# A Fourier mixing layer and a low-rank mixer in one kernel: weights and the second batch's rows asked for in another order

## The chip, the cores and the metric

The kernel runs on one core of one Trainium2 chip. The metric is the time of one launch in device microseconds (us). Three runs of the kernel before gave 485.04, 485.25 and 488.07 us; their median is 485.25 us. One further execution was taken with the hardware profiler: it took 485.87 us, of which 484.1 us lie between its first and its last instruction (the span). All times in this document that are given as a point ("at 49.10") count from the start of that span.

## The reference

For each of 8 batches, x is 3136 rows by 256 columns of float32.

```python
X = np.fft.fft(x, axis=1); X = np.fft.fft(X, axis=2)
x = X.real                                   # 8 x 3136 x 256
xt = x.transpose(0, 2, 1)
h = xt @ U @ V                               # U: 3136 x 32, V: 32 x 3136
u = x + h.transpose(0, 2, 1)
ch = np.maximum(u @ w_ch1, 0.0) @ w_ch2      # 256 -> 1024 -> 256
out = u + ch
```

## The kernel before, in words

The transforms are matrix products with tables of sines and cosines, which the kernel makes itself. The work has three stages.

**Setup.** VectorE (DVE) works out phases (helper `phase`, L184 to 188), ScalarE (ACT) takes sines of them (L190 to 200) and mirrors parts of the tables, GpSimd (POOL) mirrors others (L284). `fold_u` (L214, matmuls of L223) and `transform_u` (L239, matmuls of L249 and L262) put the columns of U into the tables.

**Folding and transforming one batch.** The rows of a batch lie in SBUF twice, in order (`xf`) and from the end (`xr`), each in two halves a = 0 and 1 of 98 partitions by 8 rows; one more partition (number 98) holds the single row of each half that has no partner. `fold` (L335) makes sums and differences: `along_d` (DVE, L319 and L321) folds the columns, `alone` (POOL, L325) copies the two columns without a partner, `mirror` (DVE, L328) joins `xf` and `xr`, `half` (DVE, L332) joins the two halves into the operand `G`. `seq` (L349, matmuls of L368) transforms along the rows, `chan` (L477, matmuls of L482 and L484) along the columns, `lowrank` and `last_row` (L489, L503) make the small operands `TA` and `VA` of the low-rank product.

**Chunks.** The 25088 rows of all batches are cut in 49 chunks of 512. `front(c)` (L521) adds the low-rank part (matmuls of L527) to the transform on DVE (L535), which gives `u`, and has `u` turned by a DMA transpose (`ut`, L538). `first_product(c, j)` (L541) multiplies by a block of `W1` (L547) and ACT applies the maximum (L549), `second_product(c, t)` (L551) multiplies by `W2` (L563), and DVE adds `ut` (L569, L571, L572) before the result is stored.

The order is written out by hand up to the loop's second chunk: everything in the setup, batch 0 and the first chunk stands in program order on each engine. The main loop (L731) issues products chunk by chunk; the steps that fold and transform batch 1 and later are spread over it by due slots (`spread`, L714): the fold of batch 1 over slots 4 to 22, its transform from slot 23 on, eight slots to a chunk. Each engine executes its own list strictly in order, so a DVE instruction that waits for a load holds back every DVE instruction behind it.

**The loads that matter here.** A DMA issued from POOL goes to one software queue, from SP to a hardware queue. Before the change POOL issues, in this order: `W1`'s first half with a cast to bfloat16 (L653), its second half as a gather in float32 to `w1t` (L55, cast later by POOL at L684), `V` (L658), `W2` with a cast (L659; the DRAM side is read in runs of 256 elements), then batch 1: `xr` half 0 (L73), `xf` half 0 (L55, a gather), `xr` half 1, `xf` half 1, and at the end the single rows of both halves of `xf` in one DMA (L77) and of `xr` in one DMA (L83). Early in the setup POOL also zeroes and fills `alt`, `TA[0]`, `TA[1]` and `VA[0]` (L172 to L182).

Of the kernel before, what the change touches and what calls it, by code (L numbers as in the profile page):

```python
# [11 lines left out]
FP32 = mybir.dt.float32  # L12
I32 = mybir.dt.int32
# [3 lines left out]
P = 128  # L17
PQ = 98
KP = PQ + 1
NI = 8  # L20
# [7 lines left out]
def kernel(  # L28
# [9 lines left out]
    nc = tc.nc  # L38
    B, S, D = x.shape
    R = moe_U.shape[1]  # L40
    H = moe_w_ch1.shape[1]
    JT = H // P
    HALF = S // 2
# [6 lines left out]
    gen = setup.enter_context(tc.tile_pool(name="gen", bufs=2))  # L50
    psum = ctx.enter_context(tc.tile_pool(name="psum", bufs=1, space=bass.MemoryType.PSUM))

    def gather(out_, t, rows, idx, w, off):

        nc.gpsimd.indirect_dma_start(  # L55
            out_, None, bass.AP(t.tensor, t.offset, [[w, rows], [1, w]]),
            bass.IndirectOffsetOnAxis(idx, 0), element_offset=off)

    def rev(t, b, a, w):

        return bass.AP(t.tensor, t.offset + (b * S + S - 784 - a * HALF) * w,
                       [[8 * w, PQ], [1, 8 * w]])

    xf = cpool.tile([KP, 2, NI, D], FP32, name="xf")
    xr = cpool.tile([KP, 2, NI, D], FP32, name="xr")

    def load_f(b, a):
        gather(xf[:PQ, a].rearrange("p i d -> p (i d)"), x, B * S // 8 - 1,
               xidx[:PQ, b, a:a + 1], 8 * D, D)

    def load_r(b, a):
        q = nc.sync if b == 0 else nc.gpsimd
        q.dma_start(out=xr[:PQ, a].rearrange("p i d -> p (i d)"), in_=rev(x, b, a, D))  # L73

    def load_0f(t, dst_f, b, w, q):
        lo = t.offset + b * S * w
        q.dma_start(out=dst_f[PQ:KP],  # L77
                    in_=bass.AP(t.tensor, lo + (NI - 1) * w,
                                [[w, 1], [HALF * w, 2], [-w, NI], [1, w]]))

    def load_0r(t, dst_r, b, w, q):
        lo = t.offset + b * S * w
        q.dma_start(out=dst_r[PQ:KP].rearrange("p a i d -> p a (i d)"),  # L83
                    in_=bass.AP(t.tensor, lo, [[w, 1], [HALF * w, 2], [1, NI * w]]))

    def load_half(b, a):
        load_f(b, a)
        load_r(b, a)
        if a == 1:
            load_0f(x, xf, b, D, nc.gpsimd)  # L90
            load_0r(x, xr, b, D, nc.gpsimd)
# [19 lines left out]
    pcol = gen.tile([P, 1], FP32, tag="pcol", name="pcol", bufs=1)  # L111
    load_0f(moe_U, UF, 0, R, nc.scalar)
    load_0r(x, xr, 0, D, nc.scalar)
    for t, n0, step in ((UF, 1, HALF), (UR, S - 784, -HALF)):
        nc.sync.dma_start(out=t[:PQ].rearrange("p a i d -> p a (i d)"),
                          in_=bass.AP(moe_U.tensor, moe_U.offset + n0 * R,
                                      [[8 * R, PQ], [step * R, 2], [1, 8 * R]]))
    load_0r(moe_U, UR, 0, R, nc.sync)
    load_r(0, 0)
    load_0f(x, xf, 0, D, nc.sync)  # L120
# [16 lines left out]
    EOF_ = cpool.tile([KP, 2, NI, 258], BF16, name="eof")  # L137
    EOR_ = cpool.tile([KP, 2, NI, 258], BF16, name="eor")
# [20 lines left out]
    W1 = cpool.tile([P, 2, H], BF16, name="w1")  # L159
    W2 = cpool.tile([P, JT, D], BF16, name="w2")  # L160
    VA = [cpool.tile([P, S], BF16, name=f"va{s}", tag=f"va{s}") for s in range(2)]
    TA = [cpool.tile([P, 256], BF16, name=f"ta{s}", tag=f"ta{s}") for s in range(2)]
    pint = cpool.tile([P, 1], I32, name="pint")
    alt = cpool.tile([P, 256], BF16, name="alt")
# [4 lines left out]
    def signs_along(t):  # L169

        v = t.rearrange("p (l two) -> p l two", two=2)
        nc.gpsimd.memset(v[:, :, 0:1], 1.0)  # L172
        nc.gpsimd.memset(v[:, :, 1:2], -1.0)

    signs_along(alt)
    for s in range(2):
        nc.gpsimd.memset(TA[s][:].bitcast(I32), 0)
        signs_along(TA[s][R:R + 2])
        nc.gpsimd.memset(TA[s][R:R + 1, :], 0.0)
        nc.gpsimd.memset(TA[s][R:R + 1, 0:1], 1.0)  # L180
        nc.gpsimd.memset(TA[s][R:R + 1, P:P + 1], -1.0)
    nc.gpsimd.memset(VA[0][:].bitcast(I32), 0)  # L182

    def phase(y, a_ap, col_ap, bits):  # L184

# [10 lines left out]
    def cosine(out_, y, bits):  # L196
        pp = y.shape[0]
        ab = gen.tile(list(y.shape), FP32, tag="ab", name="ab")
        nc.scalar.activation(ab[:], y, AF.Abs, bias=c_half[bits][:pp])
        nc.scalar.activation(out_, ab[:], AF.Sin, scale=TWO_PI / 2 ** bits, bias=c_nhp[:pp])  # L200
# [110 lines left out]
    def pin(ins):  # L311

        if PIN:
            tc.keep_in_program_order(ins)

    def along_d(a, src, dst, part):
        lo, hi = src[:, a, :, 1:128], src[:, a, :, 255:128:-1]
        if part == 0:
            pin(nc.vector.tensor_tensor(dst[:, a, :, 1:128], lo, hi, op=AL.subtract))  # L319
        else:  # L320
            pin(nc.vector.tensor_tensor(dst[:, a, :, 129:256], lo, hi, op=AL.add))  # L321

    def alone(a, src, dst):

        pin(nc.gpsimd.tensor_copy(dst[:, a, :, 128:257:128], src[:, a, :, 0:129:128]))  # L325

    def mirror(a, cols, op):
        pin(nc.vector.tensor_tensor(EOS[:, a, :, cols], EOF_[:, a, :, cols],  # L328
                                    EOR_[:, a, ::-1][:, :, cols], op=op))

    def half(b, par, cols):
        pin(nc.vector.tensor_tensor(G[b % 2][par][:, :, cols], EOS[:, 0, :, cols],  # L332
                                    EOS[:, 1, :, cols], op=AL.add if par == 0 else AL.subtract))

    def fold(b):  # L335

        for a in range(2):
            for src, dst in ((xf, EOF_), (xr, EOR_)):
                yield lambda a=a, src=src, dst=dst: (alone(a, src, dst),
                                                     along_d(a, src, dst, 0))  # L340
                yield lambda a=a, src=src, dst=dst: along_d(a, src, dst, 1)
            if b + 1 < B:
                yield lambda a=a: load_half(b + 1, a)
            yield lambda a=a: mirror(a, slice(0, 128), AL.subtract)
            yield lambda a=a: mirror(a, slice(128, 258), AL.add)
        for par in range(2):
            yield lambda par=par: half(b, par, slice(0, 258))
# [51 lines left out]
    def column_zeros():  # L399
        nc.gpsimd.memset(cf[:], 0.0)  # L400
        nc.gpsimd.memset(cr[:], 0.0)
# [87 lines left out]
    def lowrank(b):  # L489
# [3 lines left out]
        for typ in range(2):  # L493
            for par in range(2):
                nc.tensor.matmul(pt[:], d["tab"][:, typ, par, :], MDT[typ][:],  # L495
                                 start=(n == 0), stop=(n == 3 and b < B0))
# [152 lines left out]
    alone(0, xf, EOF_)  # L649
    nc.gpsimd.iota(pint[:], pattern=[[0, 1]], base=D, channel_multiplier=-1)  # L650
    nc.gpsimd.memset(pint[0:1], P)
    alone(1, xr, EOR_)
    nc.gpsimd.dma_start(out=W1[:, 0, :], in_=moe_w_ch1[0:P, :])  # L653
    w1t = gen.tile([P, H], FP32, name="w1t", tag="w1t", bufs=1)
    gather(w1t[:], moe_w_ch1, D, pint[:], H, 0)
    alone(1, xf, EOF_)
    signs_along(MSN[0:1])
    nc.gpsimd.dma_start(out=VA[0][:R, :], in_=moe_V)  # L658
    nc.gpsimd.dma_start(out=W2[:], in_=moe_w_ch2.rearrange("(j p) d -> p j d", p=P))  # L659

    for part in range(2):
        along_d(0, xr, EOR_, part)
# [6 lines left out]
        step()  # L669
    cosine(MC[:], pd[:], 17)  # L670
    MDT = [MSN, MC]
    along_d(1, xr, EOR_, 0)
    along_d(1, xf, EOF_, 0)
    mirror(1, slice(0, 128), AL.subtract)
# [2 lines left out]
    mirror(1, slice(256, 258), AL.add)  # L677
    for par in range(2):
        half(0, par, slice(256, 258))
    load_r(1, 0)  # L680
    load_f(1, 0)
    along_d(1, xr, EOR_, 1)
    load_r(1, 1)
    nc.gpsimd.tensor_copy(W1[:, 1, :], w1t[:])  # L684
    along_d(1, xf, EOF_, 1)
    mirror(1, slice(128, 256), AL.add)
    for par in range(2):
        half(0, par, slice(128, 256))
    load_f(1, 1)
    load_0f(x, xf, 1, D, nc.gpsimd)  # L690
    load_0r(x, xr, 1, D, nc.gpsimd)
    column_zeros()
    for par in range(2):
        nc.gpsimd.memset(G[1][par][:, :, 258:GW].bitcast(I32), 0)
# [24 lines left out]
    for b in range(1, B):  # L719
        hi = 8 * (b * S // CH - 1) + 2  # L720
        if b == 1:
            spread(list(fold(b)), 4, 23)
            spread(list(transform(b)), 23, hi)
        else:
            spread(list(fold(b)), hi - 66, hi - 35)
            spread(list(transform(b)), hi - 33, hi)
        if b == B0:
            spread(list(column_steps()), hi - 34, hi - 22)
# [46 lines left out]
```

## Time and profile before

| what | value |
|---|---|
| median of three runs | 485.25 us |
| the profiled execution, launch to end | 485.87 us |
| its span | 484.1 us |
| TensorE (PE) busy | 461.5 us, 95% of the span |
| DVE busy | 318.4 us, 66% |
| ACT busy | 282.6 us, 58% |
| POOL busy | 69.2 us, 14% |
| mean granted TensorE clock | 0.989 |
| DMA | 67.24 MB, mean 139 GB/s |

How to read it: a row of the timeline gives start, duration, engine, line of the kernel, operation, the output and the inputs with their shapes, and in square brackets how long the engine had been idle before and what ended that. "PEld" is TensorE's loading of weights. "SPq" or "POOLq" is an engine's queue of issued work. A row of the stage table gives for each engine the busy time and the number of instructions, then the granted TensorE clock, the mean busy share of the 16 DMA engines, and the traffic. A row of the list of DMA issues ends with the median time from issue to landing.

### The profile page before, as it was taken

Reading aid. Unit: us, or ns where it says so; the run is one execution under the profiler, and the core shown is the slowest. Engines: PE = TensorE matmul, PEld = TensorE weight load, DVE = VectorE, ACT = ScalarE, POOL = GpSimd, SP = SyncE. Lnnn points to the kernel's source line nnn. Section 1 sums busy time; section 2 is a strip of 40 time slices with the busy share of each in tenths; the row PEclk is TensorE's granted clock in tenths of the full one; section 3 lists DMA queues with packets and bytes.
Section 4 is the critical chain, followed back from the end, with each engine's and each line's share of the span. In section 5 each row is a group of like instructions: output and inputs, shape, how many; then the busy total and the mean of one; then the engine's idle time right before and its main releaser. Section 6 shows DMA issues by size and latency. Waiting matters only on the chain.

```text
span 484.1 us, 7947 instructions
## 1 busy us (share of the span) xinstructions
PE 461.5 (95%) x2979; PEld 294.9 (61%) x3033; DVE 318.4 (66%) x713; ACT 282.6 (58%) x532; POOL 69.2 (14%) x122
## 2 busy tenths in 40 slices
PE   3799799999999999999999999999999999999997
PEld 2444466665566666666666666666666666666665
DVE  8996979684668657775568657684678543434333
ACT  6826344765666556655566556655566556656562
POOL 8780421110022000130022001120000000000000
PEclk9979899999999999999999999999999999999999
DMA  7599999895266834784376725775324233343433
GB/s 209 126 207 181 160 211 172 160 184 108 66 187 182 208 66 116 182 190 130 89 196 176 182 66 144 186 205 106 88 65 118 81 85 90 86 107 96 126 89 129
DMA packets 103606, 67.24 MB, mean 139 GB/s; under 512 B 73546, under 2 KB 100068, under 8 KB 100416
## 3 DMA queue, kind: packets, MB, share of 16 engines
q1 hardware_dynamic: 97722, 40.69, 38.5%
q0 software_dynamic: 5824, 26.03, 19.9%
q8 instruction: 23, 0.38, 0.3%
q14 instruction: 15, 0.12, 0.1%
q10 hardware_dynamic: 22, 0.02, 0.0%
HBM read 29.33 MB, written 25.69 MB: 114 GB/s over the span
## 4 chain that ended last, share of the span: by engine, by line
PE 87%; DVE 7%; DMA 4%; issue 2%; POOL 0%; DVEq 0%; POOLq 0%
PE p L563 36%; PE p L547 32%; PE pt L368 9%; PE ph L527 4%; DMA xf<-in_x_dram 4%; PE pst L482 2%; PE pst L484 2%; PE ptt L495 1%; DVE eor L319 1%; PE ptc L453 1%; DVE eos L328 1%; DVE phe L188 1%; DVE pho L188 1%; DVE eof L321 0%; DVE eor L321 0%
## 5 line engine op out<-in xcount | busy, mean ns | idle before, releaser
L549 ACT ACTIVATE h<-p 128x512 bf16<-128x512 f32 x392 | 224.9, 599 | 158.3 <-PE p L547 148.8
L547 PE MATMUL p<-u,w 128*128 128x512 bf16 x732 | 209.4, 380 | 4.0 <-DVE u L535 3.1
L563 PE MATMUL p<-w,h 128*128 128x256 bf16 x1568 | 203.9, 273 | 1.5
L563 PEld LDWEIGHTS <-h 128*128 128x128 bf16 x1568 | 153.5, 98 | 60.1 <-issue 0.7
L547 PEld LDWEIGHTS <-w 128*128 128x128 bf16 x784 | 75.7, 98 | 56.8 <-DVE u L535 3.2
L569 DVE TENSOR_TENSOR o<-p,ut 128x4 f32<-128x4 f32 (+1 forms) x100 | 16.4, 164 | 92.7 <-PE p L563 87.3
L368 PEld LDWEIGHTS <-g 98*128 98x128 bf16 (+1 forms) x288 | 28.5, 99 | 28.1 <-issue 2.0
L375 DVE TENSOR_TENSOR tab<-pt,ev 128x32 bf16<-128x32 f32 x32 | 6.1, 192 | 57.5 <-PE pt L368 55.1
L55 POOL DMA_INDIRECT xf<-in_x_dram,xidx x16 | 17.9, 1120 | 167.2 <-DVE eof L321 160.8
L572 DVE TENSOR_TENSOR o<-p,ut 128x254 f32<-128x254 f32 (+1 forms) x100 | 40.8, 408 | 0.0
L571 DVE TENSOR_TENSOR o<-p,ut 128x254 f32<-128x254 f32 (+1 forms) x100 | 40.8, 408 | 0.0
L368 PE MATMUL pt<-tabc,g 98*128 98x425 bf16 (+1 forms) x160 | 35.5, 349 | 0.1
L535 DVE TENSOR_TENSOR u<-ph,S 128x512 bf16<-128x512 f32 (+15 forms) x64 | 35.1, 559 | 0.0
L535 DVE TENSOR_TENSOR u<-ph,T 128x512 bf16<-128x512 f32 (+15 forms) x64 | 35.1, 559 | 0.0
L368 PE MATMUL pt<-tabs,g 98*128 98x425 bf16 (+1 forms) x128 | 29.5, 354 | 1.1 <-DVE g L332 1.0
L527 PE MATMUL ph<-va,ta 128*128 128x512 bf16 (+13 forms) x126 | 28.9, 328 | 0.1
L372 ACT COPY ev<-pt 128x425 f32<-128x425 f32 x32 | 16.5, 516 | 21.0 <-PE pt L368 19.8
L328 DVE TENSOR_TENSOR eos<-eof,eor 99x1024 bf16<-99x1024 bf16 (+2 forms) x33 | 22.7, 702 | 0.2
L482 PE MATMUL pst<-A,mc 128*128 128x392 bf16 (+1 forms) x64 | 21.1, 330 | 0.8 <-DVE A L382 0.2
L319 DVE TENSOR_TENSOR eof<-xf 99x1016 bf16<-99x1016 f32 x16 | 19.3, 1208 | 3.8 <-DMA xf<-in_x_dram 3.8
L484 PE MATMUL pst<-B,msn 128*128 128x392 bf16 (+1 forms) x64 | 21.1, 330 | 0.0
L332 DVE TENSOR_TENSOR g<-eos 99x2064 bf16<-99x2064 bf16 (+2 forms) x20 | 19.9, 1014 | 0.1
(139 smaller groups left out, 304.3 us busy)
## 6 DMA issues: line engine op xcount, KB each, us to landing
out_dram<-o SPq DMA_DIRECT2D x48, 512.0 KB
xr<-in_x_dram POOLq DMA_DIRECT2D x14, 784.0 KB, 6.4
xr<-in_x_dram SPq DMA_DIRECT2D x2, 784.0 KB
ut<-u SPq DMA_TRANSPOSE x49
w<-in_moe_w_ch_dram POOLq DMA_DIRECT2D x1, 512.0 KB, 10.4
out_dram<-o SPq DMA_DIRECT2D x4, 128.0 KB
va<-in_moe_V_dram POOLq DMA_DIRECT2D x2, 196.0 KB, 9.1
xf<-in_x_dram,xidx POOLq DMA_INDIRECT x16, 7.2
```

Source lines behind the costliest of these rows:

```text
L319: pin(nc.vector.tensor_tensor(dst[:, a, :, 1:128], lo, hi, op=AL.subtract))
L328: pin(nc.vector.tensor_tensor(EOS[:, a, :, cols], EOF_[:, a, :, cols], EOR_[:, a, ::-1][:, :, cols], op=op))
L368: nc.tensor.matmul(pt[:], g[:kp(i), i, col:col + P], tabs[t][:kp(i), i, par, :], start=(n == 0), stop=(n == len(mm) - 1))
L482: nc.tensor.matmul(pt[:, :hi - lo], MC[:, h * P:(h + 1) * P], d["A"][:, lo:hi], start=True, stop=False)
L484: nc.tensor.matmul(pt[:, :hi - lo], MSN[:, h * P:(h + 1) * P], d["B"][:, lo:hi], start=False, stop=True)
L527: nc.tensor.matmul(ph[:, col:col + hi - lo], TA[b % 2][:, s * P:(s + 1) * P], VA[b % 2][:, lo:hi], start=True, stop=True)
L535: nc.vector.tensor_tensor(u[:, s, col:col + hi - lo], ph[:, col:col + hi - lo], src, op=AL.add)
L547: nc.tensor.matmul(p1[:], W1[:, s, j * P:(j + 1) * P], k["u"][:, s, :], start=(s == 0), stop=(s == 1))
L549: LAST[0] = nc.scalar.activation(k["h"][:, j, :], p1[:], AF.Relu)
L563: nc.tensor.matmul(p2[:, t % w, :], h[:, j, rs], W2[:, j, :], start=(j == 0), stop=(j == JT - 1))
L571: nc.vector.tensor_tensor(o[:, ts, 1:P], p2[:, :w, 1:P], ut[:, ts, 1:P], op=AL.add)
L572: nc.vector.tensor_tensor(o[:, ts, P + 1:D], p2[:, :w, P + 1:D], ut[:, tT, P - 1:0:-1], op=AL.add)
```

## The change

The edits, from first to last in program order:

1. The memsets of `alt`, `TA[0]`, `TA[1]` and `VA[0]` leave the start of POOL's list. `TA[0]` is filled between the copies `alone(1, xr)` and `alone(1, xf)`; `VA[0]` is zeroed just ahead of its load; `TA[1]` and `alt` are filled after batch 1's loads are issued.
2. `W1`'s halves are both loaded as float32 into two tiles `w1[0]` and `w1[1]`, `W2` is loaded right behind them, and all three are issued ahead of `alone(1, xr)`. `W2` is read by whole rows per partition: partition p takes rows 8p to 8p+7, 2048 elements in one run. The columns of `W1` are permuted to match.
3. ACT casts `w1[0]` and `w1[1]` to `W1`, with the permutation (a stride of 8 elements on the input), after the cosine mask `MC`. POOL's cast L684 is gone.
4. Batch 1's single rows are loaded half by half from SP's queue, four DMAs, each behind the two large loads of its half in the program. The large loads stay on POOL's queue, both of half 1 now behind `half(0, par, 128:256)` in program order.
5. The fold of batch 1 takes `xr` ahead of `xf`.

TensorE's list of instructions stays the same.

```diff
-signs_along(alt)
-for s in range(2):
+def ta_rows(s):
     nc.gpsimd.memset(TA[s][:].bitcast(I32), 0)
     signs_along(TA[s][R:R + 2])
...
-nc.gpsimd.memset(VA[0][:].bitcast(I32), 0)
...
-            for src, dst in ((xf, EOF_), (xr, EOR_)):
+            for src, dst in ((xr, EOR_), (xf, EOF_)) if b == 1 else ((xf, EOF_), (xr, EOR_)):
...
+w1 = [gen.tile([P, H], FP32, name=f"w1{s}", tag=f"w1{s}", bufs=1) for s in range(2)]
+nc.gpsimd.dma_start(out=w1[0][:], in_=moe_w_ch1[0:P, :])
+gather(w1[1][:], moe_w_ch1, D, pint[:], H, 0)
+nc.gpsimd.dma_start(out=W2.rearrange("p j d -> p (j d)"),
+                    in_=moe_w_ch2.rearrange("(p j) d -> p (j d)", p=P))
 alone(1, xr, EOR_)
-nc.gpsimd.dma_start(out=W1[:, 0, :], in_=moe_w_ch1[0:P, :])
-w1t = gen.tile([P, H], FP32, name="w1t", tag="w1t", bufs=1)
-gather(w1t[:], moe_w_ch1, D, pint[:], H, 0)
+ta_rows(0)
 alone(1, xf, EOF_)
 signs_along(MSN[0:1])
+nc.gpsimd.memset(VA[0][:].bitcast(I32), 0)
 nc.gpsimd.dma_start(out=VA[0][:R, :], in_=moe_V)
-nc.gpsimd.dma_start(out=W2[:], in_=moe_w_ch2.rearrange("(j p) d -> p j d", p=P))
...
 MDT = [MSN, MC]
+for s in range(2):
+    nc.scalar.copy(W1[:, s, :].rearrange("p (j q) -> p j q", j=JT),
+                   w1[s].rearrange("p (q j) -> p j q", j=JT))
...
-load_r(1, 0)
-load_f(1, 0)
+def load_second(a):
+    load_r(1, a)
+    load_f(1, a)
+    load_0r(x, xr, 1, D, nc.sync, a, 1)
+    nc.sync.dma_start(out=xf[PQ:KP, a, ::-1],
+                      in_=bass.AP(x.tensor, x.offset + (S + a * HALF) * D,
+                                  [[D, 1], [D, NI], [1, D]]))
+load_second(0)
 along_d(1, xr, EOR_, 1)
-load_r(1, 1)
-nc.gpsimd.tensor_copy(W1[:, 1, :], w1t[:])
 along_d(1, xf, EOF_, 1)
...
-load_f(1, 1)
-load_0f(x, xf, 1, D, nc.gpsimd)
-load_0r(x, xr, 1, D, nc.gpsimd)
+load_second(1)
+ta_rows(1)
+signs_along(alt)
 column_zeros()
```

`load_0r` takes two more arguments, the first half and the number of halves, so that it can load one half's row alone.

More of the change, by code (lines that the diff above doesn't have):

```diff
@@ L79, in load_0f, with load_0r @@
                                 [[w, 1], [HALF * w, 2], [-w, NI], [1, w]]))
[L81 to L84, printed above, removed]
+    def load_0r(t, dst_r, b, w, q, a=0, n=2):
+        lo = t.offset + (b * S + a * HALF) * w
+        q.dma_start(out=dst_r[PQ:KP, a:a + n].rearrange("p a i d -> p a (i d)"),
+                    in_=bass.AP(t.tensor, lo, [[w, 1], [HALF * w, n], [1, NI * w]]))
     def load_half(b, a):
```

## The prediction

> **What bounds the kernel now.** I read the stage table first. Its columns: stage, length, then busy time and instructions of PE, PEld, DVE, ACT and POOL, the granted clock, the DMA share.
>
> ```profile
> 26.25:41.87 15.62, 15.09 (x71) 7.17 (x72) 13.52 (x26) 4.75 (x11) 8.55 (x12) 0.89 1.02 207
> 53.42:56.94 3.52, 0.39 (x2) 0.11 (x2) 3.52 (x9) 0.00 (x0) 1.59 (x4) 1.00 0.86 208
> 56.94:66.99 10.05, 10.00 (x57) 6.18 (x58) 10.05 (x18) 4.95 (x10) 2.87 (x4) 0.83 1.04 224
> 66.99:484.10 417.11, 410.91 (x2707) 265.91 (x2755) 259.30 (x600) 244.57 (x465) 31.99 (x54) 1.00 0.54 132
> ```
>
> From 66.99 on TensorE is busy 410.9 of 417.1 us with a list that stays as it is. That stage can only be moved as a whole, by starting it earlier. What can be won lies before 66.99, where PE once stands still for 3 us while DVE is busy throughout. The timeline shows why.
>
> ```profile
> 44.65 0.68 DVE L535 TENSOR_TENSOR u<-ph,T 128x512 bf16<-128x512 f32 x1
> 49.10 1.22 DVE L319 TENSOR_TENSOR eof<-xf 99x1016 bf16<-99x1016 f32 x1 [3.77 <-DMA xf<-in_x_dram]
> 54.25 0.15 DVE L569 TENSOR_TENSOR o<-p,ut 128x4 f32<-128x4 f32 x1
> 56.34 0.39 PE L547 MATMUL p<-u,w 128*128 128x512 bf16 x1 [2.92 <-DVE u L535]
> 65.30 2.37 DVE L332 TENSOR_TENSOR g<-eos 99x2064 bf16<-99x2064 bf16 x2
> 66.99 1.61 PE L368 MATMUL pt<-tabc,g 98*128 98x425 bf16 x8
> ```
>
> DVE is free at 45.33 and waits 3.77 us for batch 1's rows. From 49.10 it works without a gap (10.05 of 10.05 us in the third stage). Chunk 2's `u` stands behind the fold, so PE waits 2.92 us for it, and `G` of batch 1 is ready at about 66.5 (half of the 2.37 behind 65.30), 17.4 us after the fold begins. PE takes it up at 66.99. The start of the fold therefore sets the start of the long stage. The chain of waits names what it waits for, and the lists of DMA issues (last column: us to landing) say how late each load was; the first two rows are the chain's and POOL's timeline.
>
> ```profile
> 31.96 17.11 DMA xf<-in_x_dram
> 26.34 1.35 POOL L55 DMA_INDIRECT xf<-in_x_dram,xidx  x1 [0.30 <-DVE g L332]
> ```
> ```profile
> w<-in_moe_w_ch_dram POOLq DMA_DIRECT2D x1, 512.0 KB, 10.4
> w1t<-in_moe_w_ch_dram,pint POOLq DMA_INDIRECT x1, 5.2
> xf<-in_x_dram,xidx POOLq DMA_INDIRECT x1, 16.1
> ```
> ```profile
> xf<-in_x_dram,xidx POOLq DMA_INDIRECT x1, 18.2
> xf<-in_x_dram POOLq DMA_DIRECT2D x1, 16.0 KB, 17.1
> ```
>
> The half that is folded first landed at 26.34 + 16.1 = 42.4, in time. Only its single row, issued last on the same queue at 31.96, came at 49.1.
>
> **The change part by part: the single rows.** They go to SP's queue, half by half. Half 0's may be issued once DVE has folded the old rows (by 21 in the timeline before). With the worst row as bound, 17.1 us, it lands by 38; half 1's, by 29 + 17.1 = 46, is wanted 7.7 us after the fold's start. Both ends are hidden, cost nothing. The large loads are issued some 1.4 us later (POOL's list, below): at 27.7 + 16.1 = 43.8 even if nothing ahead of them on the queue became shorter. So the wait goes: **-3.77 us**, and the fold starts when DVE comes to it, as 45.33 does, moved by what the setup wins.
>
> **Memsets out of the start.** The setup's chain is DVE's list up to `G`:
>
> ```profile
> 9.46 0.37 DVE L188 TENSOR_SCALAR phe<-phe 99x394 int32<-99x394 int32 x1
> 10.95 1.57 POOL L182 MEMSET va<- 128x1568 int32 x1
> 11.21 1.53 DVE L188 TENSOR_SCALAR phe<-phe 99x394 int32<-99x394 int32 x1
> 6.41 0.27 DVE L209 TENSOR_SCALAR nfl<-fl 128x256 f32<-128x256 f32 x1
> 6.72 0.92 DVE L210 TENSOR_SCALAR fl<-fl 128x256 f32<-128x256 f32 x1
> 13.38 0.59 PE L223 MATMUL pf<-ur,fl 99*99 99x256 f32 x2
> 15.26 0.67 DVE L628 CAST gu<-pf 99x512 bf16<-99x512 f32 x1
> 17.46 0.59 ACT L637 CAST gu<-pf 99x512 bf16<-99x512 f32 x1 [0.36 <-PE pf L223]
> 24.32 0.94 PE L262 MATMUL put<-sel,wu 128*98 128x64 bf16 x8 [0.58 <-ACT wu L255]
> 26.25 1.25 PE L368 MATMUL pt<-tabs,g 98*128 98x425 bf16 x3 [0.99 <-DVE g L332]
> ```
>
> Beside `VA[0]`'s memset the same operation takes 1.53 instead of 0.37: 1.16 us. L210 takes 0.92 where its like L209 takes 0.27; POOL's iotas stay beside it and only the first small memsets go, so I take half of the 0.65, 0.3. DVE wins 1.46. Two things cap it: L628 needs the matmuls that end at 13.38 + 0.59 = 13.97, and PE's next product, L368, cannot start before L262 ends at 25.26, behind ACT's chain, which waits for PE at 17.46 and so moves only with L210's 0.3, of which I keep 0.15. L368 then starts at 25.1 instead of 26.25: **-1.15 us**. The bounds are 0 (the moved memsets stretch DVE elsewhere as much) and -1.65 (L210's whole 0.65 as well).
>
> The memsets' new places: `TA[0]` (six, 1.9 us by the old ones, from 7.3 to 9.1) ahead of `alone(1, xf)`, and `VA[0]`'s 1.57 us at about 24.3, beside the L332 that makes `G`. Here are the nearest rows:
>
> ```profile
> 23.53 1.21 DVE L319 TENSOR_TENSOR eof<-xf 99x1016 bf16<-99x1016 f32 x1
> 23.62 0.24 POOL L172 MEMSET msn<- 1x128 bf16 x1
> 23.78 0.23 POOL L173 MEMSET msn<- 1x128 bf16 x1
> ```
>
> Two memsets beside a two-input DVE operation leave it at its usual 1.2 us, but they are short; L188's 1.16 is the other end. I take zero, because L332 has two inputs like L319; the 1.16 stays in the range. [...]
>
> **The clock.** A head start is worth less if PE's clock is low in it.
>
> ```profile
> 58.04 1.91 PE L563 MATMUL p<-w,h 128*128 128x256 bf16 x8
> 61.00 1.04 PE L563 MATMUL p<-w,h 128*128 128x256 bf16 x8
> ```
>
> After the stall the same eight products take 1.91 instead of 1.04. The mean clocks 0.83 over 10.05 us and 0.89 over 15.62 us both make 3.4 us at half speed, so 1.7 us lost each time. The first stretch begins where L368 does. A longer one in its place costs half of the excess; I take **+0.25**, between 0 and the 1.15 that it could eat. [...]
>
> The low stretch after the stall goes with it, but that pays little: without stall PE would be at L368 by about 61, and `G` comes 17.4 us after a fold that starts at 45.33 - 0.9 = 44.4, so at 61.8. What is late next is `G`. In the profiled execution PE came 0.4 us after `G`, a gain of that execution alone.
>
> **Weights.** POOL's three issues move into a time in which it idled:
>
> ```profile
> 19.54 0.77 POOL L325 CAST eor<-xr 99x16 bf16<-99x16 f32 x1 [2.03 <-DMA xr<-in_x_dram]
> ```
>
> They and the memsets' 1.9 + 1.57, less these 2.03, bring POOL to batch 1's loads 1.4 us later: counted above. `alone(1, xf)` is done before 24.7 and wanted by DVE near 25.4. The weights land 5.2 to 10.4 us after issue at 17 to 20, before 31; W2 is used at 46.7. Reading it by rows cannot matter below that cover. ACT gets two casts of 1024 elements:
>
> ```profile
> 16.24 0.86 ACT L296 ACTIVATE tabc<-tabs 99x784 bf16<-99x784 bf16 x1
> 26.48 0.51 ACT L200 ACTIVATE mc<-ab,c 128x256 bf16<-128x256 f32 x1
> 29.31 0.52 ACT L372 COPY ev<-pt 128x425 f32<-128x425 f32 x1 [2.31 <-PE pt L368]
> 32.33 0.89 PE L368 MATMUL pt<-tabs,g 98*128 98x425 bf16 x4
> ```
>
> 0.86 x 1024 / 784 = 1.12 each, estimated (the stride is in no row; twice that is my other end, 4.5 us for both). They run from 26.8 to 29.1; `ev` is wanted from 28.3 and is 0.8 late. PE has three buffers and needs the first back only at 32.33 - 1 = 31.3. Hidden, by 1.7 us; at the other end, 31.3, `ev`'s 0.5 would stick out. POOL's cast L684 leaves; it stood beside an L328 whose `G` PE takes up at 33.05, later than it was ready. `TA[1]`, `alt` and the fold's new order add nothing on DVE: the same operations. Batch 2's single rows are asked for about 0.6 us later relative to the fold; zero, unless DVE catches up with them.
>
> **Sum.** -3.77 - 1.15 + 0.25 = -4.67 us. From the profiled execution's 485.87 less 0.4 more: 480.8. It stands 0.62 above the median; from the median, 485.25 - 4.67 = 480.6, which I take. A run tells about 1% from no change, so 480.4 is the border.
>
> **Rivals.** *A, the loads are late anyway.* All queues share the DMA engines (share 1.02 and more in these stages); if that and not the place in the queue made the row late, it lands at 49.1 as before and the setup's gain is spent waiting: 485.2 us. Against it: its half landed at 42.4, and 16 KB took 17.1 us with all of the queue ahead of it. Chance 0.08. [...]
>
> *B, `ut` takes the wait over.* L569, at 54.25, needs chunk 0's transpose; it moves to 49.6. The packets on the hardware queue up to 50 and up to 52, both transposes:
>
> ```profile
> q1 hardware_dynamic: 875, 0.22, 60.4%
> q1 hardware_dynamic: 2136, 0.52, 69.2%
> ```
>
> At 50 not even one transpose's half of them (1068) was through. If it lands near 51 still, DVE waits 1.4 us: 482.0. Against it: they speed up as the loads end, and those end earlier. 0.12.
>
> *C, the whole setup gain*: -3.77 - 1.65, no clock loss, and 0.4 of PE's lateness: 479.4 to 479.8, say 479.6. 0.15.
>
> *D, slower*: ACT waits for `w1[1]`, with every `ev` queued behind. Issued at 18, landing after 18.2 us (the slowest gather's) at 36.2, casts done at 37.3, 6.0 after the 31.3 at which PE stalls: 485.25 - 4.67 + 6.0 = 486.6. It decides from a landing near 35 on. The row of `w1t` says 5.2. 0.03.
>
> **The numbers.** My forecast holds 0.62, with a range of its own of 479.9 to 481.3. The range 479.3 to 482.6 takes in C, B and the memset's 1.16; it leaves out A and D. Faster by over 1%: C and two fifths of the forecast, 0.40. Slower by over 1%: 0.02. Same: 0.58.
>
> **What would show it.** Right: no DVE wait for `xf` or `xr` ahead of batch 1's fold, which starts near 44.4; L188 all near 0.4; L368 near 25.1; PE at batch 1's first L368 near 61.9. Wrong: L319 of batch 1 still waiting for a DMA; a wait of L569; `ev` late with PE waiting for ACT; L332 stretched beside a memset.

## The result, and the profile after

The kernel after takes 480.92 us (median of nine runs, 480.44 to 482.17), the kernel before, timed beside it, 485.04 us (nine runs, 483.06 to 488.07). The ratio is 0.9914, with a 95% interval of 0.989 to 0.9939. That is 0.32 us above the forecast of 480.6, inside its range of 479.3 to 482.6.

The profiled execution of after took 480.92 us with a span of 479.1 us, 5.0 us less than before. The stage table of after, cut at the same events as before's (the first product on `G` of batch 0, the first product of chunk 0, the first product on `G` of batch 1):

```profile
0.00:25.01 25.01, 13.61 (x80) 9.03 (x81) 23.16 (x54) 18.71 (x31) 17.59 (x36) 0.95 0.71 200
25.01:40.89 15.88, 15.36 (x70) 7.16 (x71) 12.69 (x26) 9.18 (x15) 10.17 (x22) 0.87 0.92 207
40.89:61.81 20.92, 20.30 (x125) 12.11 (x127) 20.57 (x35) 13.83 (x27) 4.82 (x8) 1.00 1.10 193
61.81:479.10 417.29, 410.90 (x2705) 265.88 (x2756) 259.54 (x600) 244.22 (x464) 32.30 (x54) 1.00 0.54 132
```

The last stage has the same length as before (417.29 against 417.11) and the same PE time (410.90 against 410.91). It starts 5.18 us earlier. So the whole gain was made ahead of it, as the prediction had argued. (Line numbers after the fourth edit are one lower in after: L318 is before's L319, L367 is before's L368.) The timeline of after at the rows shown of before:

```profile
43.66 0.68 DVE L534 TENSOR_TENSOR u<-ph,T 128x512 bf16<-128x512 f32 x1
44.26 1.21 DVE L318 TENSOR_TENSOR eor<-xr 99x1016 bf16<-99x1016 f32 x1
49.40 0.16 DVE L568 TENSOR_TENSOR o<-p,ut 128x4 f32<-128x4 f32 x1
60.57 0.81 PE L546 MATMUL p<-u,w 128*128 128x512 bf16 x3 [0.27 <-DVE u L534]
60.44 2.36 DVE L331 TENSOR_TENSOR g<-eos 99x2064 bf16<-99x2064 bf16 x2
61.81 1.61 PE L367 MATMUL pt<-tabc,g 98*128 98x425 bf16 x8
```

There is no bracket on L318: DVE goes from `u` straight into batch 1's fold. L568 does not wait for `ut` either. PE's wait of 2.92 us for `u` is now one of 0.27. (Before, the product L527 of that `u` ended at 49.94 and DVE came to it at 55.61, after six operations of the fold.) And the setup:

```profile
6.71 0.36 DVE L209 TENSOR_SCALAR fl<-fl 128x256 f32<-128x256 f32 x1
10.30 0.37 DVE L187 TENSOR_SCALAR phe<-phe 99x394 int32<-99x394 int32 x1
13.39 0.69 DVE L627 CAST gu<-pf 99x512 bf16<-99x512 f32 x1 [0.16 <-PE pf L222]
14.13 1.52 DVE L318 TENSOR_TENSOR eor<-xr 99x1016 bf16<-99x1016 f32 x1
14.65 1.38 POOL L283 COPY tabs<-tabs 99x392 bf16<-99x392 bf16 x1
24.26 1.29 DVE L331 TENSOR_TENSOR g<-eos 99x1024 bf16<-99x1024 bf16 x2
24.55 1.40 POOL L660 MEMSET va<- 128x1568 int32 x1
25.01 1.60 PE L367 MATMUL pt<-tabs,g 98*128 98x425 bf16 x4 [0.36 <-DVE g L331]
26.28 4.03 ACT L675 CAST w<-w 128x1024 bf16<-128x1024 f32 x2
30.21 0.50 ACT L371 COPY ev<-pt 128x425 f32<-128x425 f32 x1
```

The two stretched DVE operations are back to 0.36 and 0.37 us; L627 now waits a little for PE, as the first of the prediction's two caps has it. `VA[0]`'s memset runs beside L331 without stretching it: two of them take 1.29 us, as before (at 25.50), where no memset stood beside them. ACT's two casts of `W1` take 2.0 us each, not 1.12, and `ev` comes at 30.7. PE did not wait for it.

### The profile page after: what moved, and what is told of

Same layout as the page of the kernel before. It is cut to its first block, busy times and chain, and to the rows that moved or that the text cites. A ratio compares the mean times of both kernels' runs of the same rounds, so it can differ in the third digit from the quotient of the medians.

```text
span 479.1 us, 7959 instructions
## 1 busy us (share of the span) xinstructions
PE 460.2 (96%) x2979; PEld 294.2 (61%) x3033; DVE 316.0 (66%) x713; ACT 285.9 (60%) x534; POOL 64.9 (14%) x119
## 4 chain that ended last, share of the span: by engine, by line
PE 91%; DVE 5%; DMA 2%; issue 1%; SPq 0%; DVEq 0%
PE p L562 36%; PE p L546 33%; PE pt L367 12%; PE ph L526 4%; PE pst L481 2%; DMA xf<-in_x_dram 2%; PE pst L483 2%; PE ptt L494 1%; DVE eor L318 1%; DVE eos L327 1%; DVE eof L318 1%; DVE u L534 1%; PE ptc L452 1%; DVE eor L320 1%; DVE eof L320 0%
## 5 line engine op out<-in xcount | busy, mean ns | idle before, releaser
L568 DVE TENSOR_TENSOR o<-p,ut 128x4 f32<-128x4 f32 (+1 forms) x100 | 16.4, 164 | 93.2 <-PE p L562 87.6
L367 PEld LDWEIGHTS <-g 98*128 98x128 bf16 (+1 forms) x288 | 28.5, 99 | 28.1 <-issue 2.6
L55 POOL DMA_INDIRECT xf<-in_x_dram,xidx x16 | 17.6, 1100 | 166.8 <-DVE eof L320 161.4
L367 PE MATMUL pt<-tabc,g 98*128 98x425 bf16 (+1 forms) x160 | 35.5, 349 | 0.2
L367 PE MATMUL pt<-tabs,g 98*128 98x425 bf16 (+1 forms) x128 | 29.7, 356 | 0.5 <-DVE g L331 0.4
L331 DVE TENSOR_TENSOR g<-eos 99x2064 bf16<-99x2064 bf16 (+2 forms) x20 | 19.9, 1012 | 0.1
L318 DVE TENSOR_TENSOR eor<-xr 99x1016 bf16<-99x1016 f32 x16 | 19.6, 1227 | 0.0
```

Source lines behind the costliest of these rows:

```text
L367: nc.tensor.matmul(pt[:], g[:kp(i), i, col:col + P], tabs[t][:kp(i), i, par, :], start=(n == 0), stop=(n == len(mm) - 1))
```

## The experiments

All ran with a profile and were timed against the kernel before on the same chip. In the diffs, minus is the kernel that the text names as the base.

### Which edit took DVE's wait away

My theory was the prediction's: the single row came late for its place at the end of POOL's queue, so moving the rows removes the wait and nothing else does. The rivals: the loads are late wherever they are issued; or the weights, asked for sooner, clear the queue by themselves.

**rows_only**: the kernel before with only the single rows moved.

```diff
+    load_0r(x, xr, 1, D, nc.sync, a, 1)
+    nc.sync.dma_start(out=xf[PQ:KP, a, ::-1],
+                      in_=bass.AP(x.tensor, x.offset + (S + a * HALF) * D,
+                                  [[D, 1], [D, NI], [1, D]]))
...
-    load_0f(x, xf, 1, D, nc.gpsimd)
-    load_0r(x, xr, 1, D, nc.gpsimd)
```

> The kernel before, with only the single rows of batch 1 taken half by half from SP's queue. My theory (the row was late for its place at the end of POOL's queue): batch 1's fold starts without a wait when DVE is free, at about 45.4 as in the kernel before, since the setup is not touched; G of batch 1 is taken up near 62.9, and the time is 485.0 - 3.8 = 481.2 us (480.8 to 481.8). Rival A (the shared DMA engines make the row late): DVE still waits until near 49 and the time stays at 484.5 to 485.2.

Measured: 483.81 us (482.26 to 487.44), ratio 0.9969 (0.9946 to 0.9991). DVE in its timeline:

```profile
45.57 0.68 DVE L535 TENSOR_TENSOR u<-ph,T 128x512 bf16<-128x512 f32 x1
46.17 1.21 DVE L319 TENSOR_TENSOR eof<-xf 99x1016 bf16<-99x1016 f32 x1
52.24 0.17 DVE L569 TENSOR_TENSOR o<-p,ut 128x4 f32<-128x4 f32 x1 [0.87 <-DMA ut<-u]
63.28 2.37 DVE L332 TENSOR_TENSOR g<-eos 99x2064 bf16<-99x2064 bf16 x2
```

The wait ahead of the fold is gone, but the expected 481.2 us was missed: `G` starts only 2.02 us earlier than before's 65.30. DVE was free 0.84 us later in this execution (46.17 against 45.33), and 0.87 us come back as a wait for `ut`: 3.77 - 0.84 - 0.87 = 2.06. The first comes from the clock: the granted clock was 0.50 from 21.4 to 31.7 us, where before had it from 23.0 to 29.8, and from batch 0's first product until DVE was free it took 19.89 us instead of 19.08. The second is the prediction's rival B, which after itself does not show.

**all_but_rows**: the kernel after with the single rows back at the end of POOL's queue.

```diff
-    load_second(0)
+    load_r(1, 0)
+    load_f(1, 0)
...
-    load_second(1)
+    load_r(1, 1)
+    load_f(1, 1)
+    load_0f(x, xf, 1, D, nc.gpsimd)
+    load_0r(x, xr, 1, D, nc.gpsimd)
```

> The changed kernel with batch 1's single rows back where they were: both halves in one DMA each, from POOL, behind the four large loads. My theory: the row lands right behind the last large load, which landed at 47.8 in the changed kernel, so DVE waits some 3.5 us from 44.3 on and the setup's gain is spent waiting: 484.3 us (483.6 to 485.0). A second theory (each part has its own share): the setup's 1 us stays and the time is 484.0 or less with the fold starting near 48; a third (the earlier weights alone clear the queue): the wait is under 1 us and the time under 482.

Measured: 481.86 us (481.2 to 484.38), ratio 0.9928 (0.9903 to 0.9953). POOL's copy out of the rows shows when they landed, DVE's row that nothing waits:

```profile
30.24 0.66 POOL L77 DMA_DIRECT2D xf<-in_x_dram  x1
44.34 0.26 POOL L324 CAST eor<-xr 99x16 bf16<-99x16 f32 x1 [7.95 <-DMA xr<-in_x_dram]
45.32 1.21 DVE L318 TENSOR_TENSOR eor<-xr 99x1016 bf16<-99x1016 f32 x1
```

My theory missed. The rows, still last on the same queue, landed at 44.3 instead of 49.1, one us before DVE wanted them. The third theory holds: the rest of the change, without the rows' move, clears the queue. The fold still starts 1.06 us later than in after, but not for the rows: batch 0's first product comes 0.35 us later (25.36), and the granted clock is 0.50 until 30.9 us instead of 29.1. The next two kernels ask which half of the weights' part does it.

**rows_last_plain**: all_but_rows with `W2` in its old layout (runs of 256 elements) and the casts of `W1` without a stride.

```diff
-nc.gpsimd.dma_start(out=W2.rearrange("p j d -> p (j d)"),
-                    in_=moe_w_ch2.rearrange("(p j) d -> p (j d)", p=P))
+nc.gpsimd.dma_start(out=W2[:], in_=moe_w_ch2.rearrange("(j p) d -> p j d", p=P))
...
-    nc.scalar.copy(W1[:, s, :].rearrange("p (j q) -> p j q", j=JT),
-                   w1[s].rearrange("p (q j) -> p j q", j=JT))
+    nc.scalar.copy(W1[:, s, :], w1[s][:])
```

> The kernel after with the single rows back at the end of POOL's queue, and with W2 in its old layout (1024 runs of 256 elements in place of 128 runs of 2048) and W1 cast without a stride. It tells what cleared POOL's queue in all_but_rows, where the rows landed at 44.3 instead of 49.1. Theory 1, W2's layout: W2 took 10.4 us to land by the old layout and 4.6 by whole rows; with the old one the rows come some 4 to 5 us later, at 48 to 49, DVE waits about 3.5 us for them ahead of batch 1's fold, and the time is near 485. Theory 2, the earlier place of the three issues: the rows still land near 44 to 45, DVE waits at most 0.5 us, and the time is 481.9 to 482.4. ACT's two casts: 1.1 us each if the stride is what made them 2.0, still 2.0 if it is the float32 input.

Measured: 483.76 us (480.94 to 484.7), ratio 0.995 (0.9924 to 0.9976).

```profile
27.15 1.98 ACT L674 CAST w<-w 128x1024 bf16<-128x1024 f32 x2
30.20 0.65 POOL L77 DMA_DIRECT2D xf<-in_x_dram  x1
46.05 1.22 DVE L318 TENSOR_TENSOR eor<-xr 99x1016 bf16<-99x1016 f32 x1 [0.68 <-DMA xr<-in_x_dram]
```

Issued at the same time as in all_but_rows (30.20 and 30.24), the rows land at 46.05 instead of 44.34: between these two executions the layout is worth 1.7 us. Without it the wait is 0.68, a little over theory 2's 0.5, and far from the 3.5 of theory 1. `W2` itself, issued at 19.38 and 19.40, landed 8.3 us after issue by runs of 256 and 5.6 us by whole rows. (The lists' medians of two loads, `W1`'s first half and `W2`, are 6.0 and 4.6 us; the expectation's 4.6 is the latter, of 3.6 and 5.6.) The casts take 0.99 us each, so the stride of 8 doubles them (2.0 in after). The median is 1.9 us above that of all_but_rows, more than 0.68 us of wait explains; the profiled execution, with 482.5 us, is one of the shorter ones, and what the rows did in the longer ones is not shown.

**rows_last_late**: all_but_rows with the weights issued at their old places, `W2` by whole rows.

```diff
-nc.gpsimd.dma_start(out=w1[0][:], in_=moe_w_ch1[0:P, :])
-gather(w1[1][:], moe_w_ch1, D, pint[:], H, 0)
-nc.gpsimd.dma_start(out=W2.rearrange("p j d -> p (j d)"),
-                    in_=moe_w_ch2.rearrange("(p j) d -> p (j d)", p=P))
 alone(1, xr, EOR_)
+nc.gpsimd.dma_start(out=w1[0][:], in_=moe_w_ch1[0:P, :])
+gather(w1[1][:], moe_w_ch1, D, pint[:], H, 0)
 ta_rows(0)
...
 nc.gpsimd.dma_start(out=VA[0][:R, :], in_=moe_V)
+nc.gpsimd.dma_start(out=W2.rearrange("p j d -> p (j d)"),
+                    in_=moe_w_ch2.rearrange("(p j) d -> p (j d)", p=P))
```

> The kernel after with the single rows back at the end of POOL's queue, and with the weights issued at their old places (W1 behind alone(1, xr), W2 behind V), but W2 by whole rows. Theory 1, W2's layout cleared the queue: the rows land near 45 as in all_but_rows (44.3), the wait of DVE is under 1 us, time 481.9 to 482.6. Theory 2, the earlier place did: the rows land at 48 or later, the wait is 3 us or more, time 484.5 or more.

Measured: 485.03 us (482.75 to 488.83), ratio 0.9983 (0.9957 to 1.001): the gain is gone.

```profile
27.89 0.60 POOL L660 DMA_DIRECT2D w<-in_moe_w_ch_dram  x1
32.27 0.67 POOL L77 DMA_DIRECT2D xf<-in_x_dram  x1
49.07 1.22 DVE L318 TENSOR_TENSOR eor<-xr 99x1016 bf16<-99x1016 f32 x1 [3.82 <-DMA xr<-in_x_dram]
```

Theory 2 as expected: the earlier place is what clears the queue. One reserve: with the memsets ahead of it, `W2` was issued at 27.89 here and at 24.48 before, so this kernel has the layout's gain and a later start against each other. The rows, too, were issued 2.0 us later than in all_but_rows (32.27 against 30.24), which is part of the 4.7 us by which they land later (49.07 against 44.34).

**rows_on_pool**: the kernel after with the single rows half by half, but on POOL's queue instead of SP's.

```diff
-        load_0r(x, xr, 1, D, nc.sync, a, 1)
-        nc.sync.dma_start(out=xf[PQ:KP, a, ::-1],
+        load_0r(x, xr, 1, D, nc.gpsimd, a, 1)
+        nc.gpsimd.dma_start(out=xf[PQ:KP, a, ::-1],
```

> The changed kernel with the single rows half by half from POOL's queue, each behind its own half's loads, instead of from SP. My theory (the place in the queue decides, not which queue): half 0's row lands right behind its large load, near 40 to 41, half 1's near 49, both before they are wanted (44.3 and 52 to 54): 480.9 us within 0.4. Rival (SP's queue is what helps, since it is served beside POOL's): the row takes about 17 us as before, lands near 46.5, DVE waits 2 us and the time is 483 us.

Measured: 481.42 us (480.45 to 482.62), ratio 0.9922 (0.9898 to 0.9946). The fold starts without a wait:

```profile
44.05 1.21 DVE L318 TENSOR_TENSOR eor<-xr 99x1016 bf16<-99x1016 f32 x1
```

As far as these runs can tell, SP's queue buys nothing that a place behind the row's own half on POOL's queue does not.

Put together (points of the profiled executions):

| kernel | weights early | W2 by rows | rows early | wait ahead of the fold | fold starts |
|---|---|---|---|---|---|
| before | no | no | no | 3.77 | 49.10 |
| rows_last_late | no | yes | no | 3.82 | 49.07 |
| rows_last_plain | yes | no | no | 0.68 | 46.05 |
| all_but_rows | yes | yes | no | 0 | 45.32 |
| rows_only | no | no | yes | 0 | 46.17 |
| after | yes | yes | yes | 0 | 44.26 |

The column to compare is the wait. The start of the fold also holds the setup and the clock: where there is no wait it follows how late batch 0's products ended, as said above for rows_only and all_but_rows.

### The setup

**memsets_back**: the kernel after with the memsets at POOL's start again.

```diff
+    signs_along(alt)
+    for s in range(2):
+        ta_rows(s)
+    nc.gpsimd.memset(VA[0][:].bitcast(I32), 0)
...
-    ta_rows(0)
-    nc.gpsimd.memset(VA[0][:].bitcast(I32), 0)
-    ta_rows(1)
-    signs_along(alt)
```

> The changed kernel with the memsets of alt, TA and VA[0] back at the start of POOL's list. My theory: one L187 beside VA[0]'s memset takes 1.5 instead of 0.37 us again, the first L367 starts near 26.1 instead of 25.0, the fold near 45.2 instead of 44.3, and the time is 480.9 + 0.9 = 481.8 us (481.3 to 482.3). Rival (the gain came from the weights or from the cast that left POOL, not from the memsets): 480.9 within 0.3.

Measured: 482.63 us (481.8 to 484.08), ratio 0.9936 (0.9913 to 0.996).

```profile
11.20 1.52 DVE L192 TENSOR_SCALAR phe<-phe 99x394 int32<-99x394 int32 x1
26.31 1.25 PE L372 MATMUL pt<-tabs,g 98*128 98x425 bf16 x3 [1.45 <-DVE g L336]
```

The stretched operation is back, and batch 0's first product comes at 26.31, 1.30 us behind after's 25.01. The fold starts 2.25 us later (46.51); the other 0.95 is low clock, 0.50 until 32.4 us here and until 29.1 in after. The median is 0.3 us over the expectation's upper end; its interval overlaps after's, so the size of the memsets' part, 1.30, rests on the trace.

### What sets the start of the long stage

**fold_twice**: the kernel after with one `along_d` of batch 1's fold done twice (more work for DVE, the same result).

```diff
-yield lambda a=a, src=src, dst=dst: along_d(a, src, dst, 1)
+yield lambda a=a, src=src, dst=dst: [
+    along_d(a, src, dst, 1) for _ in range(2 if b == 1 and a == 0 and src is xf else 1)]
```

> The kernel after with one along_d of batch 1's fold done twice, 1.13 us of DVE work more, the result the same. The prediction's step says that the fold of batch 1 on DVE sets the start of the long stage. If so, its G comes 1.1 us later, L367 of batch 1 at about 62.9 and the time is 1.1 us above after's. Rival: PE's own products (20.30 of 20.92 us busy) set it, and the 0.62 us in which PE stands still take up half: 0.5 us or less above after's.

Measured: 482.53 us (481.59 to 483.34), ratio 0.993 (0.9905 to 0.9955); after, timed beside it (**after_again**), 480.84 us (480.33 to 481.89), ratio 0.9894 (0.9866 to 0.9923).

> The kernel after itself, for comparison within this call: 480.9, L367 of batch 1 near 61.8. The granted clock is low for two windows of 3.41 us (mean 0.993) or three (0.989) in the setup; the prediction lets the three cost 1.7 us halved by DVE's waits at most, so executions with 0.989 should have spans 0.3 to 1.7 us longer than those with 0.993.

In both executions the fold starts at 43.69, so they can be laid on each other. First fold_twice, then after_again:

```profile
61.10 2.37 DVE L331 TENSOR_TENSOR g<-eos 99x2064 bf16<-99x2064 bf16 x2
62.47 1.61 PE L368 MATMUL pt<-tabc,g 98*128 98x425 bf16 x8
```
```profile
59.84 2.37 DVE L331 TENSOR_TENSOR g<-eos 99x2064 bf16<-99x2064 bf16 x2
61.22 1.61 PE L367 MATMUL pt<-tabc,g 98*128 98x425 bf16 x8
```

The operation done twice took 2.46 us instead of 1.21, so 1.25 us more of DVE work; `G` came 1.26 us later, PE 1.25 us later, and the median is 1.7 us higher. DVE's list sets it; the rival (half or less) is out. As to after_again's second question: over both series of after, 13 runs of after had a mean clock of 0.993 and spans of 478.6 to 479.7, two had 0.989 and spans of 480.1 and 480.4. A third low window (3.4 us more at 0.50 in all_but_rows) goes with about 1 us, by two runs.

**transform_later**: the kernel after with batch 1's transform spread from slot 26 instead of 23.

```diff
-            spread(list(fold(b)), 4, 23)
-            spread(list(transform(b)), 23, hi)
+            spread(list(fold(b)), 4, 26)
+            spread(list(transform(b)), 26, hi)
```

> The kernel after with the fold of batch 1 spread over slots 4 to 25 and its transform from slot 26 in place of 23. In the kernel after PE stands still for 0.62 us between 40.89 and 61.81 (20.30 busy of 20.92), waiting for u of chunk 3 and for G. If PE has three more slots of products in reserve while DVE ends the fold, these waits go: 480.3, 0.6 less than after. Rival: DVE, busy 20.57 of 20.92 us there, sets G's time whatever the slot, and what PE does in place of waiting it lacks elsewhere: 480.9, no change.

Measured: 481.49 us (480.09 to 482.1), ratio 0.9894 (0.9864 to 0.9924): no change, as the rival said. PE's waits for `u` went, and one for `G` came. (Its row stands later than after's 61.81 because three more slots of products run ahead of it and the setup of this execution ended later, at 25.55.)

```profile
63.46 1.60 PE L367 MATMUL pt<-tabc,g 98*128 98x425 bf16 x8 [0.51 <-DVE g L331]
```

### The clock

**busy_pe**: the kernel after with 14 matmuls of 128x512 on a tile of zeros in PE's gaps from 17.6 to 25.0; their results are not read.

```diff
+    def busy(n):
+        pz = psum.tile([P, CH], FP32, tag="p1", name="pz", bufs=3)
+        for _ in range(n):
+            nc.tensor.matmul(pz[:], wz[:, :P], wz[:], start=True, stop=True)
...
+            busy(6 if typ == 0 else 1)
```

> The kernel after with 14 matmuls of 128x512 more, on a tile of zeros whose result nobody reads, in PE's gaps from 17.6 to 25.0 of the setup (2, 6, 3, 2 and 1 at a time). In the kernel after PE was busy only about 0.9 us of the 3.4 ahead of 22.3, and its granted clock is 0.5 from 22.3 to 29.1. Theory: the low clock answers to the idle stretch just before it; with PE kept busy it stays at 1.0, the 48 matmuls of batch 0 from 25.0 take some 9.0 us instead of 10.96, and the start of the long stage moves by 1.7 to 2.0 us: 479.0 to 479.3. This is the term of the prediction that took 0.25 us off the setup's gain. Rival 1: the low stretch comes at a fixed time whatever PE does, and the 14 matmuls cost up to 0.5 us: 480.9 to 481.4. Rival 2: the clock stays up, but DVE then waits for chunk 0's transpose ut (rival B of the prediction) or for batch 1's rows, and the time is 480.3 to 480.9.

Measured: 481.69 us (480.27 to 484.25), ratio 0.9912 (0.9879 to 0.9945). Two stretches of the stage table, of after and of busy_pe; the clock is the third number from the end:

```profile
18.90:22.30 3.40, 0.89 (x17) 0.42 (x16) 3.30 (x6) 3.34 (x8) 3.09 (x4) 1.00 0.50 163
22.30:29.10 6.80, 5.86 (x26) 2.71 (x26) 6.63 (x12) 5.38 (x9) 5.96 (x15) 0.50 0.86 198
```
```profile
18.90:22.30 3.40, 3.04 (x24) 1.29 (x23) 3.30 (x5) 3.32 (x7) 3.17 (x10) 1.00 0.90 294
22.30:29.10 6.80, 6.26 (x39) 3.13 (x39) 6.63 (x12) 5.73 (x10) 5.42 (x9) 1.00 0.79 181
```

With PE busy in 3.04 of 3.40 us instead of 0.89, the low stretch of 6.8 us behind it does not occur. The kernel before has the same ahead of its low stretch: 0.88 us busy of the 3.40 from 19.6 to 23.0. How little work it takes for the clock to fall is not shown. The low clock was not the whole of it, though. Products of batch 0 and ACT in busy_pe:

```profile
26.17 4.02 ACT L687 CAST w<-w 128x1024 bf16<-128x1024 f32 x2
30.09 0.92 ACT L383 COPY ev<-pt 128x425 f32<-128x425 f32 x2
30.65 0.88 PE L379 MATMUL pt<-tabs,g 98*128 98x425 bf16 x4 [0.81 <-ACT ev L383]
61.08 1.60 PE L379 MATMUL pt<-tabc,g 98*128 98x425 bf16 x8
```

PE waits from 29.84 for `ev`, which stands behind ACT's casts. This is the prediction's "`ev` late with PE waiting for ACT": at a clock of 0.50, in after, the casts are hidden, and at 1.00 PE waits 0.81 us. From batch 0's first product to the fold it takes 18.38 us (25.16 to 43.54) against 19.25 in after, and batch 1's L379 starts 0.73 us earlier (61.08). The median shows nothing of that, and the trace says where it went: behind the last product. One of SP's last four stores takes 1.25 us to issue instead of 0.34 (minimum, median and maximum in ns; first after, then busy_pe):

```profile
L574 SPq DMA_DIRECT2D out_dram<-o x4: 332/338/345, 473.4 to 476.2; - x4
L586 SPq DMA_DIRECT2D out_dram<-o x4: 345/392/1251, 472.6 to 475.6; - x4
```

From DVE's last instruction to the end of the span it takes 3.84 us here, 2.91 in after. So the long stage is 418.22 us instead of 417.29. Why that store is issued late is open; of the 14 profiled executions only those of the two kernels with added products show it.

**busy_pe_casts_spread**: busy_pe with the casts of `W1` in eight pieces, one behind each of batch 0's steps of `seq`.

```diff
-    for step in steps[:8]:
+    for n, step in enumerate(steps[:8]):
         step()
+        s, js = n // 4, slice(n % 4 * 2, n % 4 * 2 + 2)
+        nc.scalar.copy(W1[:, s, :].rearrange("p (j q) -> p j q", j=JT)[:, js],
+                       w1[s].rearrange("p (q j) -> p j q", j=JT)[:, js])
```

> busy_pe with ACT's two casts of W1 (4.02 us in one piece, ahead of batch 0's ev) cut into eight pieces of two column blocks each, one behind each of batch 0's eight steps of seq. In busy_pe the clock stayed at 1.0, but the first ev was done only at 30.6 and PE waited 0.81 us for it; chunk 0's products began at 40.18 and not at the 38.9 that the higher clock alone would allow. Theory: the low clock was what hid the casts, and with the casts out of the way the rest of the gain comes: chunk 0's products from 39.2, batch 1's L379 from 60.1 instead of 61.81, the median 1.2 to 1.8 us under after's in the same call. Rival: something else in the chain from 25 to 60 holds as late (ut, the rows, DVE's own list): L379 of batch 1 near 61 as in busy_pe, and the median within 0.8 us of after's.

Measured: 480.4 us (479.88 to 480.64), ratio 0.9877 (0.985 to 0.9905).

```profile
14.05 0.69 DVE L639 CAST gu<-pf 99x512 bf16<-99x512 f32 x1 [0.82 <-PE pf L222]
25.66 0.90 PE L379 MATMUL pt<-tabs,g 98*128 98x425 bf16 x4 [0.48 <-DVE g L343]
43.12 1.21 DVE L330 TENSOR_TENSOR eor<-xr 99x1016 bf16<-99x1016 f32 x1
60.64 1.60 PE L379 MATMUL pt<-tabc,g 98*128 98x425 bf16 x8
```

PE's wait for `ev` is gone, and the piece from first product to fold takes 17.46 us, 1.79 less than in after. But the setup ended 0.65 us later in this execution, because `gu` waited 0.82 us for PE's first products. The median is 0.44 us under after_again's, which is the rival's number and not the 1.2 us of the theory; the intervals overlap. The same late store is part of it: one issue takes 1.25 us, and the span ends 3.87 us after DVE's last instruction. It has the lowest median of all kernels run, and the narrowest spread (0.76 us); that it is faster than after is not shown.

**casts_spread**: the same pieces in the kernel after, without the added matmuls.

> The kernel after with W1's two casts cut into eight pieces behind the steps of seq, as above, and without the added matmuls. If the casts were hidden in after, as the prediction's step says, the time is that of after within 0.3 us. If ACT's 4.03 us cost something there (ev was late by about 2 us for its PSUM buffer), it is 0.3 to 1 us less.

Measured: 482.01 us (480.56 to 482.36), ratio 0.9904 (0.9874 to 0.9934), against after_again's 0.9894. No gain, and in after PE waits for no `ev`, so after's casts are hidden. The median is 1.2 us above after_again's; the profiled execution had a late setup (25.73) and three low windows, 10.2 us (clock 0.989). From batch 0's first product to the fold it takes 19.84 us, and all_but_rows, with three low windows and the casts in one piece, 19.96: up to the fold the pieces cost nothing.

## Why the prediction was right, and where not

- **The single rows, -3.77.** The size came out: the fold starts at 44.26 (44.4 foretold), without a wait. The attribution was incomplete. "Came at 49.1 for being issued last" is right (rows_only, rows_on_pool), but the step "Reading it by rows cannot matter below that cover", with POOL's cast L684 priced at nothing, failed: it looked only at who waits for the weights, not at what is queued behind them. How much of that is L684 alone no run shows. The rows were issued 1.8 us earlier in rows_last_plain than before (30.20, 31.96) and landed 3.0 us earlier; the layout made it 4.8. The rows' move alone (rows_only) and the rest of the change without it (all_but_rows) each remove the wait, so the 3.77 may be booked to one of them, not to both.
- **Rival B** did not occur in after, but it did where the rows alone were moved (0.87 us). The argument "those loads end earlier" needed the weights out of the way, which the sum did not say.
- **Memsets, -1.15.** Measured -1.24 (26.25 to 25.01); memsets_back gives 1.30. The other end, an L331 stretched by 1.16 beside `VA[0]`'s memset, did not occur (1.29 for two). That the number came out is in part luck. The prediction let DVE win 1.46 and cut it to 1.15 because L262 would move by only 0.15. L262 (now L261) ended 0.61 earlier, at 24.65, and PE then waited 0.36 us for `G`: that cap did not hold anything up. What took its place was not foreseen: DVE stood 1.87 us ahead at L627 (15.26 to 13.39; L209 alone won 0.56, not 0.3) and gave 0.6 back, since L318 and L320 took 1.52 instead of 1.22 beside POOL's copies (the last two of L283, 1.00 and 1.38 us instead of 0.52), which had run beside other work before. So a two-input DVE operation was 0.3 us longer beside these copies and not longer beside the memset; what makes the difference no run shows. A POOL operation that began after DVE's, the cast at 17.11, left L318 at 1.22 us and took 1.24 itself; the same operation on `eor` takes 0.27 at 36.08.
- **The clock, +0.25.** Batch 0's 48 matmuls on `G` took 10.96 us instead of 10.68: 0.28. Its nature was mis-told: the low stretch does not begin where L368 does. It begins at 22.3 in after and at 23.0 in before, in the setup, after 3.4 us in which PE was busy for 0.89 and 0.88, and without it the piece up to the fold is 0.87 us shorter (busy_pe), and 1.79 with ACT's casts out of the way (busy_pe_casts_spread). That a longer low stretch costs half of its excess was the author's estimate, and no run shows the half; the runs showed stretches of 6.8 us (after) and 10.2 (all_but_rows), and two runs of after with the lower mean clock, 0.989 for 0.993, had spans about 1 us longer.
- **The casts** were mis-sized: 1.12 us each was taken and 2.0 measured (4.03 for both), close to the other end of 4.5. At that end `ev` was to stick out; it did not, since PE's low clock gave it more cover (0.50 until 29.1; at 1.00, in busy_pe, PE waited 0.81 us).
- **The last 0.4** of the profiled execution: `G` starts 4.86 earlier and PE 5.18, so 0.32.

The terms add to -3.77 - 1.24 + 0.28 - 0.32 = -5.05 where the start of the long stage moved by 5.18 and the span by 5.0. The median moved by 4.12 in the series of the result, by 5.77 in that of after_again, where before took 486.61. The ratios, 0.9914 and 0.9894, are within each other's intervals: that is how far a single series of runs fixes a change of 1%.

## What to carry to other kernels

When a load is late at the end of a software queue, list everything ahead of it, weights and issue gaps included: moving the late piece and shortening what stands ahead were the same gain here, 3.77 us, and it was had once. Price a moved load by what is queued behind it, not only by who waits for it. A cover that rests on another engine's slow clock can go when that clock is mended: the casts, hidden at 0.50, cost PE a wait of 0.81 us at 1.00. And follow a head start to the end of the span: in busy_pe 0.73 us of it reached the last product, and the stores behind that took it back (3.84 us from DVE's last instruction to the end instead of 2.91).

## What the runs showed of the hardware

In these runs PE's work starts at a low rate, 1.06 us for two matmuls of 99x256 that later take 0.59, and how long that lasts differs between executions of the same code. The last rows at the low rate and the first at the full one, in after and in all_but_rows, for the latter with DVE's wait:

```profile
11.71 0.77 PE L222 MATMUL pf<-ur,nfl 99*99 99x256 f32 x2
12.32 0.59 PE L222 MATMUL pf<-uf,nfl 99*99 99x256 f32 x2
```
```profile
13.43 0.81 PE L222 MATMUL pf<-ur,fl 99*99 99x256 f32 x2
14.07 0.59 PE L222 MATMUL pf<-uf,fl 99*99 99x256 f32 x2
14.27 0.69 DVE L627 CAST gu<-pf 99x512 bf16<-99x512 f32 x1 [1.03 <-PE pf L222]
```

Both begin at 7.37; the rate nearly doubles near 12 in one and near 14 in the other, while the granted clock of after's records reads 1.00 from 0.00 to 22.30. (In after_again, the same kernel as after, it does so near 11.) After has 6.8 us of low clock later on; all_but_rows, of mean clock 0.989, 10.2 us, from 20.7 to 30.9. The turning point sets how much of the memsets' gain arrives (what moves it no run shows): `gu` waits 0.16 us in one execution and 1.03 in the other.

The stride of 8 float32 elements on ACT's input doubled a cast of 128x1024 from 0.99 to 2.0 us.
